# Sketched attention and a rational feed-forward in one kernel: features laid out by token, the division folded into the query features, the step order written out

## The chip, the cores and the metric

The kernel runs on one core of one Trainium2 chip. Its time is device microseconds for one execution: the median of three runs. A profile of one execution lies beside it, and all views named here are of that profile.

## What is computed

The reference, cut to what matters:

```
phi(x):  a = S1 . x ; b = S2 . x            # 8 numbers each, of 32 per head
         return outer(a, b).reshape(64)
q_p, k_p = phi(q), phi(k)                   # q, k, v: 4 batches, 4 heads, 1088 tokens, 32 wide
kv  = sum over tokens of outer(k_p, v)      # 64 x 32 per batch and head
z   = sum over tokens of k_p
x   = (q_p . kv) / (q_p . z + 1e-6)         # 4352 tokens x 128 (4 heads x 32)
h   = x @ w_in                              # 128 -> 2048
P   = a0 + a1 h + a2 h^2 + a3 h^3
Q   = 1 + |b0| |h| + |b1| h^2
out = (P / (Q + 1e-6)) @ w_out              # 2048 -> 128
```

## The kernel before, in words

**Tiling.** Of the 1088 tokens of a batch, 1024 are cut into two chunks of 512 (four blocks of 128), which makes eight chunks, n = 0 to 7. The 64 tokens left of each batch form a ninth chunk of 256, the remainder. The 2048 columns of h are 16 blocks of 128; h is kept transposed, feature on the partition and token along the row. A group is some blocks of one chunk: chunk 0 has groups of 4, 4 and 8 blocks (`FIRST`), chunks 1 to 7 two groups of 8 (4096 numbers per partition), the remainder 8, 4 and 4 blocks of 256 tokens (`LAST`).

**Keys** (`add_keys`, per batch). Per chunk, TensorE transposes four 128x128 pieces of k (L286), ScalarE copies them to SBUF (L291), TensorE multiplies by S1 and S2 together (`S12`, L296), ScalarE copies the `a` half (L303), and VectorE forms the 64 products per head in four instructions, with `b` read from PSUM (L314). TensorE accumulates k_p against v with a column of ones (`v_aug`, filled by GpSimd in L271 and L272), so that kv and z come together (L328). VectorE spreads the sums into `kv_dup` and `kv_pair` (L363, L364).

**Queries** (`add_queries`, per chunk). q is transposed (L379, L384). `Srep` expands the transposed q to `a` and to `b` repeated 64 times, features on the partition, two heads at a time (L389, a 64-row matmul); ScalarE copies the `a` side (L394), VectorE multiplies (L398): `q_pT`. TensorE forms numerators and denominators by token (L405), VectorE adds 1e-6, takes the reciprocal and multiplies (L415 to L417), TensorE transposes x (L424), ScalarE copies it (L428).

**Feed-forward** (`add_group`, per group g). h by f32 matmuls, two blocks into each of two PSUM buffers of 1024 (L466); ScalarE copies to bf16 `hb` (L472); VectorE makes |h| (L476, `m`), |b1| |h| + |b0| (L482, `u`) and u m (L486); ScalarE takes 1/Q as exp(-ln(1 + 1e-6 + u)) in pieces of 2048 (L490, L495, `r`); VectorE makes a3 h + a2 (L499, `y`), times h (L503), plus a1 (L506), times h (L503 again), times r (L510). TensorE adds two terms into the output, r against a0 w_out and y against w_out (L517), which `weights` has scaled and converted on VectorE (L258, L259). After the last group of a chunk the output is copied, transposed and stored (L522, L527, L532, L574; the remainder's four stores L580).

**Order.** Every engine carries out its instructions in the order in which they were issued. `Plan` holds steps with an engine, an assumed duration, predecessors, a rank and the buffers that they take and give; `issue` simulates them greedily with a fixed `HOP` of 190 ns between engines and issues them by start time. All loads are on SP's queue, in the order k0, S1/S2, v0, k remainders, v remainders, q0, a and b, w_in (L174), w_out (L175), then the rest (the digit is the batch). Buffers: `hb` three, `m` one, `u`, `r` and `y` two, `L` two, `xT` three, `w_ps` (PSUM for all small products) two.

The same helper makes every matmul into `w_ps`, so a line of the profile stands for one step kind. An f32 matmul appears as two records of TensorE, an f32 transpose or a bf16 matmul as one.

Of the kernel before, what the change touches and what calls it, by code (L numbers as in the profile page):

```python
# [17 lines left out]

class Plan:

    HOP = 190
# [5 lines left out]
    def add(self, engine, ns, fn, after=(), rank=0.0, take=(), give=(), lag=0):  # L30
        s = dict(engine=engine, ns=ns, fn=fn, after=[a for a in after if a is not None], rank=rank,
                 take=take, give=give, lag=lag, end=None, n=len(self.steps))
        self.steps.append(s)
        return s

    def issue(self):
        todo = list(self.steps)
        free_at = {}
        pool = {k: [0] * v for k, v in self.bufs.items()}
        done = []  # L40
        while todo:
            best = None
            for s in todo:
                if any(a["end"] is None for a in s["after"]):
                    continue
                t = free_at.get(s["engine"], 0)
                for a in s["after"]:
                    t = max(t, a["end"] + (a["lag"] if a["engine"] == s["engine"] else self.HOP + a["lag"]))
                blocked = False
                for b in s["take"]:  # L50
                    if not pool[b]:
                        blocked = True
                        break
                    t = max(t, min(pool[b]))
                if blocked:
                    continue
                key = (t, s["rank"], s["n"])
                if best is None or key < best[0]:
                    best = (key, s)
# [5 lines left out]
            for b in s["give"]:  # L65
                pool[b].append(s["end"] + self.HOP)
            todo.remove(s)
            done.append(s)
        for s in sorted(done, key=lambda s: (s["start"], s["n"])):
            s["fn"]()  # L70
# [4 lines left out]
def kernel(  # L75
# [28 lines left out]
    FR = 1.45  # L104
    GW = GF * CW
    FIRST = [4, 4, 8]
    LAST = [8, 4, 4]
# [15 lines left out]
    BUFS = dict(xT=3, hb=3, m=1, u=2, r=2, y=2, L=2, h_ps=2, out_ps=1, w_ps=2, kv_ps=1,  # L123
                k_sb=2, v_sb=2, q_sb=2, v_aug=2, kT=2, a_t=2, k_p=2, qT=2, A_sb=2, q_pT=2, den=2, x=2,
# [3 lines left out]

    k_rem = big.tile([128, B // 2, H, D], FP, name="k_rem")
    v_rem = big.tile([128, B // 2, H, D], FP, name="v_rem")
    q_rem = big.tile([128, B // 2, H, D], FP, name="q_rem")

    def load_main(name, src, b):
        t = io.tile([128, H, J, D], FP, name=name, bufs=BUFS[name])
        T[name, b] = t
        nc.sync.dma_start(out=t, in_=src[b, :, 0:MAIN, :].rearrange("h (p j) d -> p h j d", j=J))

    def load_rem(dst, src):  # L140
        for b in range(B):
            nc.sync.dma_start(out=dst[(b % 2) * REM:(b % 2 + 1) * REM, b // 2, :, :],
                              in_=src[b, :, MAIN:S, :].rearrange("h p d -> p h d"))

# [4 lines left out]
    w_out_l = moe.tile([128, LW], FP, name="L", bufs=BUFS["L"])  # L149
    w_out_f = w_out_l.rearrange("p (n d) -> p n d", d=d_model)  # L150

    def load_small():
        for i, s in enumerate((S1, S2)):
            nc.sync.dma_start(out=SR[i * R:(i + 1) * R, :, :],
                              in_=bass.AP(tensor=s.tensor, offset=s.offset, ap=[[D, R], [0, H], [1, D]]))

    def load_ab():
        nc.sync.dma_start(out=a_sb, in_=bass.AP(tensor=moe_a.tensor, offset=moe_a.offset,
                                                ap=[[0, 128]] + list(moe_a.ap)))
        nc.sync.dma_start(out=b_sb, in_=bass.AP(tensor=moe_b.tensor, offset=moe_b.offset,  # L160
                                                ap=[[0, 128]] + list(moe_b.ap)))

    def load(fn, ns, n=1, **kw):
        return plan.add("SP", 650 * n, fn, lag=ns, **kw)

    ld = {}
    ld["k", 0] = load(lambda: load_main("k_sb", k, 0), 4000, rank=-99, take=["k_sb"])
    ld["s"] = load(load_small, 2000, 2, rank=-98)
    ld["v", 0] = load(lambda: load_main("v_sb", v, 0), 4500, rank=-97, take=["v_sb"])
    ld["kr"] = load(lambda: load_rem(k_rem, k), 2500, 4, rank=-96)  # L170
    ld["vr"] = load(lambda: load_rem(v_rem, v), 2500, 4, rank=-95)
    ld["q", 0] = load(lambda: load_main("q_sb", q, 0), 4000, rank=-94, take=["q_sb"])
    ld["ab"] = load(load_ab, 2000, 2, rank=-93)
    ld["wi"] = load(lambda: nc.sync.dma_start(out=w_in_sb, in_=moe_w_in), 8000, rank=-92)  # L174
    ld["wo"] = load(lambda: nc.sync.dma_start(out=w_out_f, in_=moe_w_out.rearrange("(fo fi) d -> fi fo d", fi=128)),  # L175
                    9000, rank=-91, take=["L"])
    for i, (name, src) in enumerate((("k", k), ("v", v), ("q", q))):
        ld[name, 1] = load(lambda name=name, src=src: load_main(name + "_sb", src, 1), 6000, rank=-90 + i,
                           take=[name + "_sb"])
    ld["qr"] = load(lambda: load_rem(q_rem, q), 3000, 4, rank=-80)  # L180
    for b in range(2, B):
        for i, (name, src) in enumerate((("k", k), ("v", v), ("q", q))):
            ld[name, b] = load(lambda name=name, src=src, b=b: load_main(name + "_sb", src, b), 5000, rank=-70 + i,
                               take=[name + "_sb"])
# [5 lines left out]
    mask2 = consts.tile([128, 2], FP, name="mask2")  # L190
    one_ap = consts.tile([128, 1], FP, name="one_ap")

    kv_dup = big.tile([128, B, H, 2 * (D + 1)], FP, name="kv_dup")
    kv_pair = big.tile([128, B, NP, 2 * (D + 1)], FP, name="kv_pair")
    v_rem_aug = big.tile([128, B // 2, H, D + 1], FP, name="v_rem_aug")
# [3 lines left out]
    wide = [consts.tile([128, R, R], FP, name=f"wide{i}") for i in range(2)]  # L199
    Srep = [consts.tile([128, 2, R * R], FP, name=f"Srep{i}") for i in range(2)]  # L200
    W_terms = [big.tile([128, NF, d_model], BF, name=f"w_out_{i}") for i in range(2)]

    def pool_consts():
# [3 lines left out]
        for h in range(H):  # L207
            nc.gpsimd.memset(mask4[h * D:(h + 1) * D, h:h + 1], 1.0)
            nc.gpsimd.memset(mask2[h * D:(h + 1) * D, h % 2:h % 2 + 1], 1.0)
        nc.gpsimd.memset(one_ap, 1.0 + 1e-6)  # L210

    def pool_zero():
        nc.gpsimd.memset(kv_dup, 0.0)
        nc.gpsimd.memset(kv_pair, 0.0)
# [4 lines left out]

# [3 lines left out]
    def first_warm():  # L223
        warm_ps.append(ops.tile([128, CW], FP, name="out_ps", bufs=1))
        warm(8)

    c_zero = plan.add("DVE", 250, lambda: nc.vector.memset(zeros, 0.0), rank=-99)
    c_pool = plan.add("POOL", 2000, pool_consts, rank=-99)
    c_kv0 = plan.add("POOL", 1500, pool_zero, rank=-98)
    c_warm = plan.add("PE", 3500, first_warm, after=[c_zero], rank=-99, take=["out_ps"])  # L230

    def s_transpose():
        T["sT"] = aps.tile([128, CW], FP, name="w_ps", bufs=BUFS["w_ps"])
        nc.tensor.transpose(T["sT"][:, :2 * R], in_=SR.rearrange("r h d -> r (h d)"), identity=ident[:2 * R, :2 * R])

    def s_spread():
        nc.vector.tensor_copy(out=sT, in_=T["sT"][:, :2 * R])
        nc.vector.tensor_mul(out=S12, in0=sT[:, None, :].broadcast_to([128, H, 2 * R]),
                             in1=mask4[:, :, None].broadcast_to([128, H, 2 * R]))

    def s_rep():
        for i in range(2):
            src = sT[:, 0:R, None] if i == 0 else sT[:, None, R:2 * R]
            nc.vector.tensor_copy(out=wide[i], in_=src.broadcast_to([128, R, R]))
            nc.vector.tensor_mul(out=Srep[i],
                                 in0=wide[i].rearrange("p i j -> p (i j)")[:, None, :].broadcast_to([128, 2, R * R]),
                                 in1=mask2[:, :, None].broadcast_to([128, 2, R * R]))

    c_sT = plan.add("PE", 250, s_transpose, after=[ld["s"], c_pool], rank=-98, take=["w_ps"])
    c_s12 = plan.add("DVE", 450, s_spread, after=[c_sT], rank=-98, give=["w_ps"])  # L250
    c_rep = plan.add("DVE", 1100, s_rep, after=[c_s12], rank=-97)
# [5 lines left out]
    def weights():  # L257
        nc.vector.tensor_scalar(out=W_terms[0], in0=w_out_f, scalar1=a_sb[:, 0:1], scalar2=None, op0=AX.mult)  # L258
        nc.vector.tensor_copy(out=W_terms[1], in_=w_out_f)  # L259

    c_b = plan.add("DVE", 100, abs_b, after=[ld["ab"]], rank=-5)
    c_w = plan.add("DVE", 2500, weights, after=[ld["ab"], ld["wo"]], rank=-0.25, give=["L"])


    def add_keys(b, rank):
        warm_n = 1 if b == 0 else 0
        last = {}

        def v_ones():
            T["va", b] = io.tile([128, H, J, D + 1], FP, name="v_aug", bufs=BUFS["v_aug"])  # L270
# [3 lines left out]
        va = plan.add("POOL", 1300, v_ones, after=[ld["v", b]], rank=rank, take=["v_aug"], give=["v_sb"])  # L274
        if b == 0:
            def vr_ones():
                nc.gpsimd.memset(v_rem_aug[:, :, :, D:D + 1], 1.0)
                nc.gpsimd.tensor_copy(out=v_rem_aug[:, :, :, 0:D], in_=v_rem)

            T["vr_step"] = plan.add("POOL", 600, vr_ones, after=[ld["vr"]], rank=rank)  # L280

        def features(key, srcs, n, after, rank, give=(), keep=False):
            def transposes():
                T["kTp", key] = aps.tile([128, CW], FP, name="w_ps", bufs=BUFS["w_ps"])
# [4 lines left out]
            def evac():  # L289
                T["kT", key] = att.tile([128, CW], FP, name="kT", bufs=BUFS["kT"])  # L290
                nc.scalar.copy(out=T["kT", key][:, :n * 128], in_=T["kTp", key][:, :n * 128])  # L291

            def project_ab():
                T["ab", key] = aps.tile([128, CW], FP, name="w_ps", bufs=BUFS["w_ps"])
# [359 lines left out]
```

## Time and profile before

| what | value |
|---|---|
| median of 3 runs | 324.46 us (323.81, 324.46, 333.47) |
| profiled execution, its span | 323.9 us |
| TensorE busy | 280.0 us (86%) |
| VectorE busy | 286.5 us (88%) |
| ScalarE busy | 228.4 us (71%) |
| GpSimd busy | 8.7 us (3%) |
| mean granted TensorE clock | 0.954 |
| moved by DMA | 11.20 MB |

The page gives no time of its own for the profiled execution beside its span; against the median of the runs the span is 0.6 us shorter, which is what lies around it. Busy time is counted per engine, and the shares are of the whole span, over stages with different limits. PE is TensorE, PEld its weight loads, DVE VectorE, ACT ScalarE, POOL GpSimd, SP the queue of loads and stores.

### The profile page before, as it was taken

How to read it: one execution, taken by the hardware profiler on the slowest of the kernel's cores; microseconds unless marked ns; L12 is line 12 of the kernel's file. 1: busy time of each engine (PE TensorE's matmuls, PEld its weight loads, DVE VectorE, ACT ScalarE, POOL GpSimd, SP SyncE). 2: the span in 40 equal slices, each digit the busy share in tenths (PEclk: the TensorE clock that was granted, in tenths of full speed). 3: DMA queues.
4: the chain of work that ended last, by engine and by line, in shares of the span. 5: the costliest groups of instructions: out<-in, count | busy, mean ns of one | idle time of the engine just before them, and what ended most of it. 6: DMA issues, size and time to landing. Idle time of an engine off the chain costs nothing.

```text
span 323.9 us, 3027 instructions
## 1 busy us (share of the span) xinstructions
PE 280.0 (86%) x1153; PEld 150.0 (46%) x1172; DVE 286.5 (88%) x300; ACT 228.4 (71%) x213; POOL 8.7 (3%) x29
## 2 busy tenths in 40 slices
PE   7969999988899999898999998979999975992532
PEld 4835455555443544555445554645345422650220
DVE  1461599999999999999999999999999999999990
ACT  3122678979479879794798888675989795686650
POOL 4102000002000000000000000000000000000000
PEclk9997999999999999999999999989999999698695
DMA  5798000200020000000000000000000000000000
GB/s 157 222 314 266 0 1 2 65 1 0 25 74 0 0 34 0 0 0 2 32 0 1 34 0 0 0 2 32 0 0 35 0 0 0 0 34 0 0 32 16
DMA packets 12125, 11.20 MB, mean 35 GB/s; under 512 B 4048, under 2 KB 10448, under 8 KB 11984
## 3 DMA queue, kind: packets, MB, share of 16 engines
q1 hardware_dynamic: 12112, 11.02, 11.2%
q8 instruction: 9, 0.15, 0.2%
q14 instruction: 4, 0.03, 0.0%
HBM read 8.79 MB, written 2.23 MB: 34 GB/s over the span
## 4 chain that ended last, share of the span: by engine, by line
DVE 77%; PE 13%; DMA 5%; issue 1%; SPq 1%; ACT 1%; DVEq 0%
DVE y L503 22%; DVE u L486 11%; DVE y L510 10%; DVE y L499 6%; DVE u L482 6%; DVE y L506 6%; PE h_ps L466 6%; DVE m L476 5%; DMA L<-in_moe_w_out_dram 3%; DVE q_pT L398 3%; DVE k_p L314 2%; PE out_ps L517 2%; PE w_ps L405 2%; DMA v_sb<-in_v_dram 2%; PE w_ps L389 2%; DVE x_sb L417 2%
## 5 line engine op out<-in xcount | busy, mean ns | idle before, releaser
L466 PE MATMUL h_ps<-xT,w_in_sb 128*128 128x512 f32 (+1 forms) x288 | 127.7, 584 | 2.7 <-ACT xT L428 2.4
L472 ACT CAST hb<-h_ps 128x1024 bf16<-128x1024 f32 x68 | 67.7, 1013 | 23.6 <-PE h_ps L466 22.8
L490 ACT ACTIVATE L<-u,one_ap 128x2048 f32<-128x2048 bf16 (+1 forms) x35 | 68.4, 1954 | 18.1 <-DVE u L486 18.1
L503 DVE TENSOR_TENSOR y<-y,hb 128x4096 bf16<-128x4096 bf16 (+2 forms) x40 | 78.9, 1972 | 1.2
L466 PEld LDWEIGHTS h_ps<-xT,w_in_sb 128*128 128x128 f32 x288 | 53.3, 194 | 56.3 <-issue 42.3
L495 ACT ACTIVATE r<-L 128x2048 bf16<-128x2048 f32 (+1 forms) x35 | 65.4, 1870 | 0.4
L517 PE MATMUL out_ps<-r,w_out_108 128*128 128x512 bf16 (+1 forms) x139 | 35.6, 378 | 11.6 <-ACT r L495 11.2
L517 PE MATMUL out_ps<-y,w_out_109 128*128 128x512 bf16 (+1 forms) x132 | 34.4, 389 | 10.7 <-DVE y L510 9.9
L486 DVE TENSOR_TENSOR u<-u,m 128x4096 bf16<-128x4096 bf16 (+2 forms) x20 | 39.4, 1971 | 0.6
L510 DVE TENSOR_TENSOR y<-y,r 128x4096 bf16<-128x4096 bf16 (+2 forms) x20 | 39.3, 1965 | 0.1
L517 PEld LDWEIGHTS <-w_out_109 128*128 128x128 bf16 x144 | 14.4, 104 | 32.1 <-issue 21.7
L517 PEld LDWEIGHTS <-w_out_108 128*128 128x128 bf16 x144 | 14.2, 102 | 32.1 <-issue 22.6
L476 DVE TENSOR_SCALAR m<-hb 128x4096 int16<-128x4096 int16 (+2 forms) x20 | 21.2, 1060 | 7.5 <-ACT hb L472 7.5
L482 DVE TENSOR_SCALAR u<-m,b_abs 128x4096 bf16<-128x4096 bf16 (+2 forms) x20 | 23.7, 1185 | 0.6
L499 DVE TENSOR_SCALAR y<-hb,a_sb 128x4096 bf16<-128x4096 bf16 (+2 forms) x20 | 23.6, 1181 | 0.0
L506 DVE TENSOR_SCALAR y<-y,a_sb 128x4096 bf16<-128x4096 bf16 (+2 forms) x20 | 22.5, 1126 | 0.7
L405 PE MATMUL w_ps<-kv_dup,q_pT 128*128 128x66 f32 x128 | 16.9, 288 | 5.4 <-DVE q_pT L398 5.4
L405 PEld LDWEIGHTS w_ps<-kv_dup,q_pT 128*128 128x128 f32 x128 | 16.6, 204 | 9.7 <-DVE q_pT L398 7.7
L328 PEld LDWEIGHTS kv_ps<-v_aug,k_p 128*128 128x128 f32 x128 | 16.3, 191 | 3.2 <-issue 1.9
L394 ACT COPY A_sb<-w_ps 128x512 f32<-128x512 f32 (+1 forms) x18 | 9.5, 564 | 10.7 <-PE w_ps L389 10.7
L389 PE MATMUL w_ps<-qT,Srep_106 64*128 64x512 f32 (+1 forms) x36 | 16.9, 615 | 0.1
L328 PE MATMUL kv_ps<-v_aug,k_p 128*128 128x66 f32 x128 | 16.2, 269 | 0.1
(70 smaller groups left out, 184.0 us busy)
## 6 DMA issues: line engine op xcount, KB each, us to landing
k_sb<-in_k_dram SPq DMA_DIRECT2D x4, 512.0 KB, 4.0
v_sb<-in_v_dram SPq DMA_DIRECT2D x4, 512.0 KB, 5.8
q_sb<-in_q_dram SPq DMA_DIRECT2D x4, 512.0 KB, 3.9
out_dram<-oT SPq DMA_DIRECT2D x8, 256.0 KB, 2.0
w_in_sb<-in_moe_w_in_dram SPq DMA_DIRECT2D x1, 1024.0 KB, 7.1
k_rem<-in_k_dram SPq DMA_DIRECT2D x4, 32.0 KB, 4.4
v_rem<-in_v_dram SPq DMA_DIRECT2D x4, 32.0 KB, 2.7
q_rem<-in_q_dram SPq DMA_DIRECT2D x4, 32.0 KB, 6.4
```

The source lines that it names most:

```text
L405: nc.tensor.matmul(nd_ps[r0:r1, i * 66:(i + 1) * 66], lhsT=T["q_pT", n, hp][:, i * 128 + r0:i * 128 + r1], rhs=kv_of(b, i, hp), start=True ...
L466: nc.tensor.matmul(T["h", g, s][:, i * W:(i + 1) * W], lhsT=w_in_sb[:, fi * 128:(fi + 1) * 128], rhs=T["xT", n][:, :W], start=True, stop=True)
L472: nc.scalar.copy(out=T["hb", g][:, s * W:(s + nsub) * W], in_=T["h", g, s])
L482: nc.vector.tensor_scalar(out=T["u", g][:, :gw], in0=T["m", g][:, :gw], scalar1=b_abs[:, 1:2], scalar2=b_abs[:, 0:1], op0=AX.mult, op1=AX.add)
L486: nc.vector.tensor_mul(out=T["u", g][:, :gw], in0=T["u", g][:, :gw], in1=T["m", g][:, :gw])
L490: nc.scalar.activation(out=T["L", g, l0][:, :lw], in_=T["u", g][:, l0:l0 + lw], func=ACT.Ln, bias=one_ap)
L495: nc.scalar.activation(out=T["r", g][:, l0:l0 + lw], in_=T["L", g, l0][:, :lw], func=ACT.Exp, scale=-1.0)
L499: nc.vector.tensor_scalar(out=T["y", g][:, :gw], in0=T["hb", g][:, :gw], scalar1=a_sb[:, 3:4], scalar2=a_sb[:, 2:3], op0=AX.mult, op1=AX.add)
L503: nc.vector.tensor_mul(out=T["y", g][:, :gw], in0=T["y", g][:, :gw], in1=T["hb", g][:, :gw])
L506: nc.vector.tensor_scalar(out=T["y", g][:, :gw], in0=T["y", g][:, :gw], scalar1=a_sb[:, 1:2], scalar2=None, op0=AX.add)
L510: nc.vector.tensor_mul(out=T["y", g][:, :gw], in0=T["y", g][:, :gw], in1=T["r", g][:, :gw])
L517: nc.tensor.matmul(T["o", n][:, :W], lhsT=W_terms[t][:, fis[i], :], rhs=src[:, i * W:(i + 1) * W], start=(t == 0 and fis[i] == 0), stop=(t ...
```

## The change

**Queries by token.** q is transposed and copied as before, and then multiplied block by block by `W_abc`, 24 columns per head: S1, S2, and S2 times z reshaped, built per batch from z (`z_blocks`, `z_project`, `z_spread`; the S columns are put there by GpSimd in `s_weights`). So a token's row holds a, b and c, where a . c is the denominator. One ScalarE copy takes all of them to SBUF; VectorE forms a . c (`scale`: multiply, reduce, add 1e-6, reciprocal) and multiplies a by 1/den, and one instruction makes the 64 products of every head (`product`). TensorE transposes them back (eight 128x128 transposes, `p_transposes`), ScalarE copies them, and `x_mm` multiplies with the block-diagonal `kv_bd` as the stationary side, so that x comes out transposed; `x_mm` of head pair hp writes 64 partitions from hp * 64. Chunk 0 is made `early`: features by token without c, numerators, division and x transposes as before.

**Keys by token.** One ScalarE copy brings a and b of all four blocks to SBUF, and one instruction makes the products of a chunk (1024 numbers per partition) in place of four.

**Feed-forward.** `u` is multiplied in place, Exp writes over `u`, and `lin` takes the place of `m`; there is no `r`. `u` has three buffers, `lin` one. In even groups from g = 2 on (`THREE`), the addition of a1 is left out: hb times u goes into `hb`, y times hb into `y`, and TensorE adds a third term, hb against a1 w_out. `FIRST` is 2, 2, 4, 8 blocks, `LAST` 8, 4, 2, 2.

**Weights and loads.** a0 w_out and w_out are converted by GpSimd, a1 w_out by ScalarE. k0 is loaded in two halves; ScalarE's queue takes the first k and v remainders, a and b, and two of the last four stores.

**Order.** `ORDER`, a list of all 726 steps, is issued as written. By step, SP's queue begins

```
q0 | k0 first half | S1,S2 | k1 | k0 second half | v0 | q1 | q rem 0 | w_out | v rem 1 | v1 | k2 | w_in | v3 | k rem 1 | q3 | ...
```

and TensorE's and VectorE's queues hold, around groups 4 to 7 (`pr`, `pg`, `py` are the three terms of the output; n1, n2, n4, n5 the steps of y; * a three-term group):

```
PE:  ... h 6,6 | qptr 3,1 | pr 4,2048 | h 7,2 | h 7,0 | pg 4* | qtr 4 | kv 20 | py 4 | ktr 30 | pr 5,0 | h 7,4 | h 7,6 | ...
DVE: ... umul 5 | n4 4* | abs 6* | n4 5 | lin 6* | n5 4* | umul 6* | n5 5 | n1 6 | k product 31 | n2 6 | abs 7 | n1 7 | ...
```

The diff, cut to its core:

```diff
-    HOP = 190
+    HOP = dict(PE=220, ACT=110, DVE=110, POOL=160, SP=100)
+    SELF = dict(PE=0, ACT=60, DVE=90, POOL=60, SP=0)
...
     def issue(self):
+        if ORDER:
...
+            for i in ORDER:
...
+                self.steps[i]["fn"]()
+            return
...
-    FIRST = [4, 4, 8]
-    LAST = [8, 4, 4]
+    FIRST = [2, 2, 4, 8]
+    LAST = [8, 4, 2, 2]
+    THREE = lambda g: g >= 2 and g % 2 == 0
...
-    BUFS = dict(xT=3, hb=3, m=1, u=2, r=2, y=2, L=2, h_ps=2, out_ps=1, w_ps=2, kv_ps=1,
-                k_sb=2, v_sb=2, q_sb=2, v_aug=2, kT=2, a_t=2, k_p=2, qT=2, A_sb=2, q_pT=2, den=2, x=2,
+    BUFS = dict(xT=3, hb=3, u=3, lin=1, y=2, L=2, h_ps=2, out_ps=1, w_ps=2, kv_ps=1,
+                k_sb=2, v_sb=2, q_sb=2, v_aug=2, kT=2, ab=2, k_p=2, qT=2, abc=2, q_p=1, q_pT=2, den=2,
...
+    def s_weights(b):
+        for h in range(H):
+            nc.gpsimd.tensor_copy(out=W_abc[:, b, h, :, 0:2 * R], in_=S12)
+        for i in range(b, B, 2):
+            nc.gpsimd.tensor_copy(out=W_rem[:, i, :, 0:2 * R], in_=S12)
...
-        nc.vector.tensor_scalar(out=W_terms[0], in0=w_out_f, scalar1=a_sb[:, 0:1], scalar2=None, op0=AX.mult)
-        nc.vector.tensor_copy(out=W_terms[1], in_=w_out_f)
+    c_w0 = plan.add("POOL", 2300, lambda: nc.gpsimd.tensor_scalar(
+        out=W_terms[0], in0=w_out_f, scalar1=a_sb[:, 0:1], scalar2=None, op0=AX.mult),
+        after=[ld["ab"], ld["wo"]], rank=-4)
+    c_w1 = plan.add("POOL", 2300, lambda: nc.gpsimd.tensor_copy(out=W_terms[1], in_=w_out_f), after=[ld["wo"]], rank=-3.9)
+    c_w2 = plan.add("ACT", 1900, lambda: nc.scalar.activation(
+        out=W_terms[2].rearrange("p n d -> p (n d)"), in_=w_out_l, func=ACT.Copy, scale=a_sb[:, 1:2]),
...
+                nc.vector.tensor_mul(out=k_p, in0=ab[:, :, 0:R, None].broadcast_to([128, n * H, R, R]),
+                                     in1=ab[:, :, None, R:2 * R].broadcast_to([128, n * H, R, R]))
...
+        def kv_blocks():
+            nc.vector.tensor_mul(out=kv_bd[:, b, :, 0:2 * D].rearrange("p n (h d) -> p n h d", h=2),
+                                 in0=kv_of()[:, :, :, 0:D],
+                                 in1=mask2[:, None, :, None].broadcast_to([128, NP, 2, D]))
...
+        def z_blocks():
+            nc.vector.tensor_mul(out=z_bd[:, b], in0=kv_of()[:, :, 0, D:D + 1].broadcast_to([128, NP, 2 * R]),
+                                 in1=mask16[:, None, :].broadcast_to([128, NP, 2 * R]))
...
+            nc.tensor.matmul(T["zp", b][:, :H * R], lhsT=S2x, rhs=z_bd[:, b].rearrange("p n c -> p (n c)"),
+                             start=True, stop=True)
...
+                nc.vector.tensor_mul(out=W_abc[:, b % 2, :, :, 2 * R:R3], in0=z[:, :, None, :].broadcast_to([128, H, JC, R]),
+                                     in1=mask4[:, None, :, None].broadcast_to([128, H, JC, R]))
...
+        def project():
+            T["abcp", n] = tile_of(aps, "w_ps", [128, CW], FP)
+            for (c0, c1, g0, w) in weights():
+                r0 = c0 % 128
+                nc.tensor.matmul(T["abcp", n][r0:r0 + c1 - c0, g0 * RC:(g0 + 4) * RC], lhsT=T["qT", n][:, c0:c1],
+                                 rhs=w.rearrange("p g r -> p (g r)"), start=True, stop=True)
...
+        def scale():
...
+            nc.vector.tensor_mul(out=pr, in0=abc[:, :, 0:R], in1=abc[:, :, 2 * R:R3])
+            nc.vector.tensor_reduce(out=den, in_=pr, axis=mybir.AxisListType.X, op=AX.add)
+            nc.vector.tensor_scalar(out=den, in0=den, scalar1=1e-6, scalar2=None, op0=AX.add)
+            nc.vector.reciprocal(out=den, in_=den)
+            nc.vector.tensor_mul(out=abc[:, :, 0:R], in0=abc[:, :, 0:R], in1=den.broadcast_to([128, G, R]))
...
+        def x_mm(hp):
...
+            for (c0, c1, w) in kv_lhs(hp):
+                nc.tensor.matmul(T["xTp", n][hp * 64:(hp + 1) * 64, c0:c1], lhsT=w[:, 0:2 * D],
+                                 rhs=T["q_pT", n][:, hp, c0:c1], start=True, stop=True)
...
+        if terms == 2:
+            p = plan.add("DVE", ts, n_add, after=[p], rank=g - 0.3, name=f"n3 {g}")
+            p = plan.add("DVE", tt, mul(y, y, hb), after=[p], rank=g - 0.3, give=["hb"], name=f"n4 {g}")
+            p = plan.add("DVE", tt, mul(y, y, u), after=[p, e], rank=g + 0.55, name=f"n5 {g}")
...
+        else:
+            r = plan.add("DVE", tt, mul(hb, hb, u), after=[p, e], rank=g + 0.5, name=f"n4 {g}")
+            p = plan.add("DVE", tt, mul(y, y, hb), after=[r], rank=g + 0.55, name=f"n5 {g}")
+            o = plan.add("PE", pj, lambda: project("hb", 2, 0, len(fis), False, False), after=[r, rt, c_w], rank=g + 0.55,
+                         give=["u"], name=f"pg {g}")
+            o = plan.add("PE", pj, lambda: project("y", 1, 0, len(fis), False, final), after=[p, o], rank=g + 0.56,
+                         give=["hb", "y"], name=f"py {g}")
...
-            nc.sync.dma_start(out=out[b * S + MAIN:(b + 1) * S, :],
-                              in_=oT[(b % 2) * REM:(b % 2 + 1) * REM, b // 2, :])
+            (nc.sync if b % 2 == 0 else nc.scalar).dma_start(
+                out=out[b * S + MAIN:(b + 1) * S, :], in_=oT[(b % 2) * REM:(b % 2 + 1) * REM, b // 2, :])
```

## The prediction, made before the changed kernel ran

> **What bounds the kernel now.** First the page's busy table and its 40 slices.
>
> ```profile
> span 323.9 us, 3027 instructions
> PE 280.0 (86%) x1153; PEld 150.0 (46%) x1172; DVE 286.5 (88%) x300; ACT 228.4 (71%) x213; POOL 8.7 (3%) x29
> PE   7969999988899999898999998979999975992532
> DVE  1461599999999999999999999999999999999990
> ```
>
> VectorE (DVE) has little to do for four slices and is then full to the end: its idle time is the start and the last few us. But TensorE (PE) is nearly full too, until the last eight slices. How nearly is read from busy time by window, in two chunks of the steady part with one batch of keys:
>
> ```profile
> core 0: us, PE busy (x) PEld busy (x) DVE busy (x) ACT busy (x) POOL busy (x), PEclk, DMA share, GB/s
> 131.00:197.00 66.00, 62.90 (x262) 33.42 (x266) 65.04 (x64) 52.60 (x51) 0.00 (x0) 1.00 0.02 9
> ```
>
> DVE 98.5%, PE 95.3%, ScalarE (ACT) 80%. A saving on DVE alone can thus give at most some 5% here. Next the timeline of the start:
>
> ```profile
> 9.93 0.43 SPq L174 DMA_DIRECT2D w_in_sb<-in_moe_w_in_dram  x1
> ...
> 20.54 1.29 DVE L258 TENSOR_SCALAR w_out_108<-L,a_sb 128x2048 bf16<-128x2048 f32 x1 [2.27 <-DMA L<-in_moe_w_out_dram]
> ...
> 23.00 1.29 DVE L398 TENSOR_TENSOR q_pT<-A_sb,w_ps 128x512 f32<-128x512 f32 x2
> ...
> 30.98 7.13 PE L466 MATMUL h_ps<-xT,w_in_sb 128*128 128x512 f32 x16
> ...
> 35.77 0.69 DVE L476 TENSOR_SCALAR m<-hb 128x2048 int16<-128x2048 int16 x1 [7.49 <-ACT hb L472]
> ```
>
> The feed-forward stream of DVE starts at 35.77: the weight copies (L258, L259) wait for w_out and hold up q_pT, and so x and h. From 35.7 to 316.5 DVE is busy 275.15 of 280.8 us (98.0%); 7.4 us follow. So the span is 35.8 + 280.7 + 7.4, and I price the three parts.
>
> **DVE work, whole run.** Rows by form (mean ns last before the second bar):
>
> ```profile
> L506 DVE TENSOR_SCALAR y<-y,a_sb 128x4096 bf16<-128x4096 bf16 x15 | 19.3, 1286 | 0.5
> L314 DVE TENSOR_TENSOR k_p<-a_t,w_ps 128x256 f32<-128x256 f32 x32 | 11.2, 415 | 1.2 <-ACT a_t L303 1.2
> L398 DVE TENSOR_TENSOR q_pT<-A_sb,w_ps 128x512 f32<-128x512 f32 x16 | 10.3, 683 | 0.1
> L245 DVE TENSOR_TENSOR Srep_107<-wide_105,mask_96 128x128 f32<-128x128 f32 x1 | 0.3, 293 | 0.0
> ```
>
> Third term: n_add (L506) goes in seven groups of 4096 (9.0 us), two of 2048 (0.75 each) and one of 512 (about 0.35): -10.9. Finer first and last groups: a two-term group of 1024 costs 4.76 us over its eight rows, one of 2048 7.96, so two for one is +1.56; at 512, by the slope between 1024 and 2048, 3.15, so +1.54: +3.1. Key products: L398 gives 1.05 ns per element (683 at 512, 414 at 256), so one product of 1024 takes 1.22; eight are 9.8 against 11.2: -1.4. Queries: lines 398 and 415 to 417 go, 25.0 in all their forms; new per later chunk are two multiplies of 128 elements (0.29, L245), the reduction, an addition (0.16) and a reciprocal (0.20) as before, and a product of 1.22. No row shows a reduction; it lies between a 64-wide copy (0.22) and twice the multiply (0.58); I take 0.29 because it reads as many elements. That is 2.45 times seven, 2.8 for chunk 0 (old division), 1.7 for the remainder: 21.7, so -3.3 (+2 at the upper bound). kv: twelve copies of 0.22 per two batches become four or five multiplies per batch: 5.4 to 4.3, -1.1. Weights and Srep gone, S2x copied: -3.2. Sum -16.8: 269.7 us. Of this about 10.4 lies before the stream (five key products, query 0, S and kv blocks) where it was 11.36, so 259.3 us follow.
>
> In the two-chunk window: -2.57 (n_add), -0.4, -0.8, -0.3: DVE 65.04 to 61.0.
>
> **PE work, the same window.** Rows of that window:
>
> ```profile
> L389 PE MATMUL w_ps<-qT,Srep_106 64*128 64x512 f32 x8 | 4.5, 641 | 0.0
> L405 PE MATMUL w_ps<-kv_dup,q_pT 128*128 128x66 f32 x32 | 3.9, 275 | 0.6 <-DVE q_pT L398 0.6
> L389 PE MATMUL w_ps<-qT,Srep_107 64*128 64x512 f32 x8 | 2.4, 635 | 0.0
> L424 PE MATMUL w_ps<-ident,x_sb 128*128 128x128 f32 x8 | 1.2, 276 | 0.1
> ```
>
> These 12.0 us go (an f32 matmul is two records). Added: 8 projections of 96 columns at 0.29 (64 columns, L296, take 0.26): 2.3; 16 transposes of q_p at 0.15: 2.4; one z projection 0.3; the third term, 16 bf16 matmuls at the 0.216 between starts of L517: 3.5. The last is x_mm, four f32 matmuls 64 outputs wide on 512 columns. L389, half an array high, shows both ends: two halves one after the other 1.05 us each, both together 1.06. Which holds for half-width tiles is shown by the remainder's numerators, which write 64 outputs each into alternating halves:
>
> ```profile
> L405 PE MATMUL w_ps<-kv_pair,q_pT 128*64 128x66 f32 x16 | 0.7, 228 | 0.0
> ```
>
> 0.044 us a record against 0.12 for the full-width ones: halves run together. The new order puts the two x_mm of most chunks side by side, so I take 2.1 (two pairs), 4.2 as the other end. PE 62.9 - 12.0 + 10.6 = 61.5 (or 63.6). So **the third term hands PE what the shorter query path saved**, and DVE and PE become equal.
>
> [...]
>
> **How fast a window becomes.** DVE at today's 98.5%: 62.0 us. PE at today's 95.3%: 64.5, or 66.7 with 63.6. Two equal engines wait for each other more than one behind a full one, so I take 64.5. ACT gains an evacuation of 384 elements per chunk (about 0.48; 512 take 0.59) and 0.1 per key chunk: 54 of 64.5, inside its gaps. Cover gone, it would cost that 0.6 a chunk.
>
> **The start.** On SP's queue the order is q0, half of k0, S1/S2, k1, the other half, v0, q1, one q remainder, w_out, a v remainder, v1, k2, and only then w_in: 5.5 MiB with itself, about 6.0 MB with the remainders. k2 waits for k_sb, which the transposes of k0 free by about 9, earlier than the bandwidth. DMA moved 231 and 283 GB/s in 2 to 6 us and 305 to 347 in 14 to 22: 1.0 MB by 6 us and 5.0 at 310 give w_in at about 22 (21 to 25), later than today's 17.0. What else h waits for: v0 (2 MiB) at about 9.7, its copy 11, key sums to 16, numerators, two divisions of 0.8, transposes and evacuation, about 21. So w_in ends last. The k and v remainders and a, b are issued by ACT (six issues, 0.6 each on SP today) while it has nothing to evacuate (until 6.10 today); the k remainder, first in PE's order, lands at 7 to 8, under v0's 11. The third weight copy (2048 wide, about 1.9 as L495) falls in ACT's wait for w_in. The other two copies go to POOL; w_out lands near 16 and its first copy takes 2 to 4 us (v_aug: 1.04 for half as many elements), ahead of the W_abc copies (about 2) that z_spread waits for on DVE: 20 to 22, under w_in; from 25 on it would be late, and the stream behind it with it. h at 22.0, and the first 1024 columns evacuated 3.05 us later, as now (30.98 to 34.02): **the stream starts at 25.1, not 35.8**.
>
> **The end.** 7.4 us: the last projection halves (-0.4), and four stores whose issue took 2.46 on one queue go by two (-1.2): 5.8.
>
> **Sum.** 25.1, plus 3.5 windows of 64.5 (225.8), plus the other 259.3 - 3.5 x 61.0 = 45.8 us of DVE at 98% (46.7), plus 5.8: 303.4 against 323.9. The median of the runs lies 0.6 above that span, so about **304**; its own range is 294 (DVE sets the window, w_in at 21) to 314 (66.7, w_in at 25).
>
> **Rivals.**
> (1) PE becomes the bound: x_mm one after the other, 63.6 a window at 95.3%: 3.5 x 2.2 = 8 us more, **312**. For: PE has no slack left. Against: the kv_pair row.
> (2) The start gives nothing, because w_in behind k2, or the W_abc copies behind POOL's weight copies, come as late as x does today: 304 + 10.7 = **315**. Against: 5.5 MiB at any rate seen after 14 us.
> (3) Slower: the hold on hb. A three-term group writes hb times u into hb and needs it until n5, where today the second L503 releases it; with three hb the evacuation for group g+3 waits for that, and ACT's Ln behind it, and PE's h. In the new order 9.4 us of DVE work lie between n5 of group 4 and abs of group 7, and in that time PE must do py 4 (1.8), a key transpose (0.6), a projection (0.9) and two h of 1.72, and ACT the last evacuation: 8.3 us. From 1.1 us of delay on DVE stands still; 4 us in each of seven groups make 28, **332**. For: PE full and in order. Against: DVE's only wait for hb now is the first, 7.5 us.
> (4) The gains add undisturbed, 62.0 a window or better: **294** or below.
>
> **How the numbers follow.** Forecast 0.55, (1) 0.16, (2) 0.08, (3) 0.13, (4) 0.08. A difference under 2% is about what cannot be told from none; the bounds are 318 and 331. The forecast, (4), and most of (1) and (2) lie under 318: 0.77; same takes 0.12, from what is left of (1) and (2) and a half-paid (3); slower 0.11, the rest of (3). The range, 293 to 321, leaves out the slower half of (3) and the tail of (4).
>
> **What would show it.** First DVE work on h near 25 us; w_in landing last before h; a two-chunk window of 64 to 65 us with PE and DVE both at 94 to 96%; pairs of x_mm in about 1.1 us; DVE busy about 270 us. I am wrong on the mechanism if PE idles over 10% in the middle while DVE waits for hb, or if DVE stays over 98% and yet takes 66 us a window.

## The result, and the profile after

The changed kernel takes **308.97 us** (median; 304.52 to 310.27), the kernel before beside it 324.13: ratio **0.948** [0.939, 0.957]. Run again unchanged later (`e12`), it took 305.97 us, ratio 0.941 [0.936, 0.947]. The profiled execution of the changed kernel took 310.27 us, the slowest of its four, and that of `e12` 305.65; the table gives both. The forecast was 304 us: faster, as expected, and near. But two of its three terms were wrong, in opposite directions:

| part of the span | before | forecast | after | `e12` |
|---|---|---|---|---|
| to the first VectorE work on h | 35.8 | 25.1 | 43.4 | 42.3 |
| the stream, to the last step of y | 280.7 | 272.5 | 259.1 | 255.9 |
| the end | 7.4 | 5.8 | 5.8 | 5.6 |
| span | 323.9 | 303.4 | 308.3 | 303.7 |

The start became 8 us longer instead of 11 shorter; the stream, which is VectorE's part from the first work on h to the last step of y, lost 21.6 us instead of 8.2. The page of the changed kernel ("after" from here on), busy table and slices:

```profile
span 308.3 us, 3083 instructions
PE 287.0 (93%) x1189; PEld 163.1 (53%) x1189; DVE 268.5 (87%) x253; ACT 234.9 (76%) x228; POOL 16.9 (5%) x45
...
PE   5999999999999999999999999999999997977962
...
DVE  0237349999999999999999999999999998999892
```

VectorE now has little to do for six slices, and TensorE counts as busy in all of them but the first. What TensorE does there shows in the timeline of the start (start, duration, engine, line; in brackets what the engine waited for):

```profile
18.42 0.38 ACTq L212 DMA_DIRECT2D a_sb<-in_moe_a_dram  x1
18.59 3.52 PE L396 MATMUL kv_ps<-v_aug,k_p 128*128 128x66 f32 x16
...
23.38 5.44 POOL L320 TENSOR_SCALAR w_out<-L,a_sb 128x2048 bf16<-128x2048 f32 x1 [11.11 <-DMA a_sb<-in_moe_a_dram]
...
23.78 5.06 DVE L316 TENSOR_SCALAR b_abs<-b_sb 128x2 int32<-128x2 int32 x1 [2.42 <-DMA b_sb<-in_moe_b_dram]
...
38.59 3.76 PE L616 MATMUL h_ps<-xT,w_in_sb 128*128 128x512 f32 x4
...
43.43 0.55 DVE L653 TENSOR_SCALAR y<-hb,a_sb 128x1024 bf16<-128x1024 bf16 x1 [3.09 <-ACT hb L622]
```

Three things are to be seen. The 16 key sums take 3.52 us, where `e12` does the same 16 in 1.90, and the four records of h 3.76, where they take 1.88 later on: TensorE runs at half rate. The load of a is issued only at 18.42, and GpSimd's copy of a0 w_out waits for it. And `b_abs`, two numbers per partition, takes 5.06 us beside that copy (0.17 before). In the stream the picture is the reverse; busy time by window, and after it VectorE's waits between 60 and 290 us (us in total, times, longest):

```profile
core 0: us, PE busy (x) PEld busy (x) DVE busy (x) ACT busy (x) POOL busy (x), PEclk, DMA share, GB/s
131.00:197.00 66.00, 65.73 (x289) 35.18 (x288) 65.31 (x62) 60.43 (x57) 0.00 (x0) 1.00 0.02 9
```

```profile
DVE y L653 <- PE out_ps L662: 1.3, 2, 1.0
```

Both engines stand at 99%, and VectorE waits 1.3 us for others in 230. The first y step of the 4096-wide groups starts at 155.95 and, two chunks (four groups) later, at 218.59: **62.6 us for two chunks**. Before, the same distance was 66.2 (160.57 to 226.76).

### The profile page after: what moved, and what is told of

It reads as the page before. It is cut to its first block, busy times and chain, and to the rows that moved or that the text cites. A ratio compares the mean times of both kernels' runs of the same rounds, so it can differ in the third digit from the quotient of the medians.

```text
span 308.3 us, 3083 instructions
## 1 busy us (share of the span) xinstructions
PE 287.0 (93%) x1189; PEld 163.1 (53%) x1189; DVE 268.5 (87%) x253; ACT 234.9 (76%) x228; POOL 16.9 (5%) x45
## 4 chain that ended last, share of the span: by engine, by line
DVE 47%; PE 43%; issue 4%; ACT 3%; DMA 2%; DVEq 0%
DVE y L642 18%; PE h_ps L616 14%; PE out_ps L662 12%; DVE u L642 6%; DVE lin L638 5%; PE kv_ps L396 5%; DVE y L653 5%; DVE hb L642 4%; DVE u L633 4%; PE w_ps L362 3%; DVE y L656 2%; DVE q_p L515 2%; DMA k_rem<-in_k_dram 2%; PE w_ps L479 1%; PE w_ps L352 1%
## 5 line engine op out<-in xcount | busy, mean ns | idle before, releaser
L622 ACT CAST hb<-h_ps 128x1024 bf16<-128x1024 f32 (+1 forms) x69 | 68.4, 999 | 24.5 <-PE h_ps L616 21.3
L616 PEld LDWEIGHTS h_ps<-xT,w_in_sb 128*128 128x128 f32 x288 | 53.9, 197 | 48.4 <-issue 39.5
L642 DVE TENSOR_TENSOR y<-y,hb 128x4096 bf16<-128x4096 bf16 (+3 forms) x44 | 78.7, 1798 | 0.1
L646 ACT ACTIVATE L<-u,one_ap 128x2048 f32<-128x2048 bf16 (+2 forms) x37 | 69.2, 1870 | 6.6 <-DVE u L642 6.2
L649 ACT ACTIVATE u<-L 128x2048 bf16<-128x2048 f32 (+2 forms) x37 | 65.8, 1779 | 0.3
L662 PEld LDWEIGHTS <-w_out 128*128 128x128 bf16 x358 | 35.5, 100 | 57.2 <-issue 31.1
L662 PE MATMUL out_ps<-y,w_out 128*128 128x512 bf16 (+1 forms) x144 | 34.7, 381 | 5.5 <-DVE y L642 5.5
L662 PE MATMUL out_ps<-u,w_out 128*128 128x512 bf16 (+1 forms) x144 | 36.7, 383 | 3.4 <-ACT u L649 3.4
L642 DVE TENSOR_TENSOR u<-lin,u 128x4096 bf16<-128x4096 bf16 (+3 forms) x22 | 39.6, 1799 | 0.1
L653 DVE TENSOR_SCALAR y<-hb,a_sb 128x4096 bf16<-128x4096 bf16 (+3 forms) x22 | 24.2, 1098 | 5.9 <-ACT hb L622 3.1
L638 DVE TENSOR_SCALAR lin<-u,b_abs 128x4096 bf16<-128x4096 bf16 (+3 forms) x22 | 24.1, 1097 | 0.1
L362 PEld LDWEIGHTS w_ps<-S,kT 128*128 128x128 f32 x68 | 12.6, 262 | 2.3 <-issue 1.5
```

The lines of the kernel that those rows point to most:

```text
L362: nc.tensor.matmul(T["abp", key][:, i * 64:(i + 1) * 64], lhsT=T["kT", key][:, i * 128:(i + 1) * 128], rhs=S12.rearrange("p h r -> p (h r) ...
L616: nc.tensor.matmul(T["h", g, s][:, i * W:(i + 1) * W], lhsT=w_in_sb[:, fi * 128:(fi + 1) * 128], rhs=T["xT", n][:, :W], start=True, stop=True)
L622: nc.scalar.copy(out=T["hb", g][:, s * W:(s + nsub) * W], in_=T["h", g, s][:, :nsub * W])
L638: nc.vector.tensor_scalar(out=lin(), in0=u(), scalar1=b_abs[:, 1:2], scalar2=b_abs[:, 0:1], op0=AX.mult, op1=AX.add)
L642: return lambda: nc.vector.tensor_mul(out=out(), in0=in0(), in1=in1())
L646: nc.scalar.activation(out=T["L", g, l0][:, :lw], in_=T["u", g][:, l0:l0 + lw], func=ACT.Ln, bias=one_ap)
```

## The experiments

**`e12`, `e10`, `e1`, `e5`: what holds the start.** `e12` is the changed kernel unchanged, once more. `e10` only issues a and b right behind the first remainders on ScalarE's queue, ahead of its evacuations; `e1` only doubles the dummy matmuls of the start; `e5` does both.

In short (the steps of the queue by name; a and b are one step):

```diff
 e1, e5:  first_warm:  -        warm(7)
                       +        warm(14)
 e10, e5: ORDER, ACT:  - k rem 0 | v rem 0 | eight evacuations | a, b | ...
                       + k rem 0 | v rem 0 | a, b | eight evacuations | ...
```

> The first run of dummy matmuls is 14 long in place of 7, so that it bridges the gap until the k remainder arrives (4.43 to 6.56 us in the profile of the changed kernel). Theory A (clock): the changed kernel's start is late because TensorE's matmuls run at half rate from 6.56 to 42 us (16 key-sum records take 3.5 us where the kernel before took 1.9); with the gap bridged the first of them are at full rate, the feed-forward stream of VectorE starts at 28 to 35 us in place of 43.4, and the time falls by 5 to 12 us to about 297. Theory B (loads and waits): the start hangs on the k remainder, v0, and a, b behind GpSimd's weight copy; then the stream still starts at 41 to 44 and the time stays within 3 us of 307.

> The 14 first dummy matmuls, and a and b are loaded on ScalarE's queue right behind the first remainders, in place of behind nine evacuations; nothing else. In the kernel with the 14 alone, the block-diagonal kv copies on VectorE end at 23.33 us, when GpSimd's 5.44 us weight copy ends, and TensorE stands for 3.1 us before the numerators and is then at half rate. Theory A (the late a, b): VectorE's b_abs no longer waits, GpSimd's copy starts when w_out lands (about 17), the kv copies come at 20 or, still held by the copy, at 22.6; stream at 28 to 34, time 296 to 303. Theory B (only the copy on GpSimd counts, not when a and b arrive): the kv copies are held to 22.5 or later, stream at 34 to 35.5, within 1.5 us of the kernel with the 14 alone (303).

> The changed kernel with a and b loaded early and nothing else: the first dummy matmuls stay 7 long. Theory A (the clock is the larger loss, and the late a, b count only behind it): matmuls at half rate from 6.6 to about 40 us as in the changed kernel, stream at 40 to 43, time 304 to 307. Theory B (the late a, b are the loss, and the half rate only follows from the wait that they cause): stream at 28 to 34, time 294 to 300.

> The changed kernel once more, unchanged, to see whether the same list of instructions starts at the same clock each time. Theory A (the clock's release in the first 45 us is a matter of chance, since the kernel with early a and b had it at 13 us and the changed kernel's profile not before 42): the executions spread over 5 us or more, 302 to 309, more than those of the kernels with a bridged gap (1.1 to 1.8 us with early a and b). Theory B (each list of instructions has one start): the executions agree within 2 us.

| kernel | median us (lowest to highest) | ratio to before | stream starts | stream |
|---|---|---|---|---|
| after | 308.97 (304.52 to 310.27) | 0.948 [0.939, 0.957] | 43.4 | 259.1 |
| `e12` | 305.97 (304.84 to 309.71) | 0.941 [0.936, 0.947] | 42.3 | 255.9 |
| `e1` | 303.24 (301.85 to 303.67) | 0.927 [0.918, 0.935] | 35.5 | 258.8 |
| `e10` | 296.78 (295.37 to 309.61) | 0.913 [0.906, 0.921] | 30.4 | 258.8 |
| `e5` | 294.37 (293.66 to 295.36) | 0.910 [0.907, 0.912] | 28.4 | 258.7 |

The start moves by 15 us, and the stream behind it stays at 256 to 259: the two terms add, as in the sum of the prediction. The second theory for `e10` came true. `e5` started where its first theory said and was 1.6 us faster than that theory's range; `e1` fell between its two theories, and so did `e12`, whose six executions spread over 4.9 us. `e12` shows how the loads of a and b hold the start, even where the keys run at full rate. Its timeline and, behind it, its windows:

```profile
15.90 0.36 ACTq L212 DMA_DIRECT2D a_sb<-in_moe_a_dram  x1
15.90 1.90 PE L396 MATMUL kv_ps<-v_aug,k_p 128*128 128x66 f32 x16
...
24.53 5.44 POOL L320 TENSOR_SCALAR w_out<-L,a_sb 128x2048 bf16<-128x2048 f32 x1 [11.94 <-DMA v_sb<-in_v_dram]
24.94 5.05 DVE L316 TENSOR_SCALAR b_abs<-b_sb 128x2 int32<-128x2 int32 x1 [6.11 <-DMA b_sb<-in_moe_b_dram]
...
30.15 3.65 PE L541 MATMUL w_ps<-kv_bd,q_pT 128*128 128x66 f32 x16 [7.68 <-DVE kv_bd L440]
...
38.14 3.04 PE L616 MATMUL h_ps<-xT,w_in_sb 128*128 128x512 f32 x4
...
42.27 0.55 DVE L653 TENSOR_SCALAR y<-hb,a_sb 128x1024 bf16<-128x1024 bf16 x1 [2.37 <-ACT hb L622]
```

```profile
24.00:32.00 8.00, 1.85 (x9) 1.88 (x10) 5.05 (x3) 2.00 (x1) 7.47 (x9) 0.67 0.02 4
32.00:40.00 8.00, 8.00 (x34) 6.96 (x34) 4.44 (x11) 1.33 (x3) 3.35 (x11) 0.50 0.00 0
```

a is issued at 15.90 and lands 8.5 us later by the DMA view, among the large loads (the page names v as what the copy waited for; a landed last). Copy and `b_abs` then end together at 30 (in after, `e1` and `e2` too they end within 0.03 us of each other, however late `b_abs` began), `kv_bd` is queued behind `b_abs` on VectorE, TensorE stands for 7.68 us and comes back at a granted clock of 0.50, at which what leads to h takes about twice as long (numerators 3.65 us, 1.97 in `e5`; transposes of x 1.06, 0.61 in `e5`). In `e5` the same rows read:

```profile
16.76 0.17 DVE L315 TENSOR_SCALAR b_abs<-b_sb 128x2 int32<-128x2 int32 x1
...
18.48 5.44 POOL L319 TENSOR_SCALAR w_out<-L,a_sb 128x2048 bf16<-128x2048 f32 x1 [4.66 <-DMA L<-in_moe_w_out_dram]
...
20.00 0.29 DVE L435 TENSOR_TENSOR kv_bd<-kv_ps,mask 128x128 f32<-128x128 f32 x1 [3.08 <-PE kv_ps L395]
...
25.31 1.96 PE L615 MATMUL h_ps<-xT,w_in_sb 128*128 128x512 f32 x4
...
28.36 1.85 DVE L652 TENSOR_SCALAR y<-hb,a_sb 128x1024 bf16<-128x1024 bf16 x1 [1.31 <-ACT hb L621]
```

`b_abs` is done ahead of the copy, `kv_bd` runs in its usual 0.29 beside it, and h begins at 25.31 in place of 38. `e10` shows that the early a and b do most of it alone (stream at 30.4, 12 us before `e12`); the dummies alone bring 6.8 us of the start and 2.7 of the time (`e1`, 303.24 beside `e12`'s 305.97), because there `b_abs` still ends with the copy, at 23.3, TensorE still stands 3.1 us, and its first h records still take 3.76. What is **not settled** is why the keys ran at half rate in after's profiled execution and at full rate in `e12`'s, which issues the same instructions: with seven dummies the executions spread widely (304.5 to 310.3; one run of `e10` at 309.61 among three at 295 to 297), with fourteen under 2 us in `e1` and `e5` but over 8 in `e2`, below. So it varies by execution, and the number of dummies alone doesn't settle it.

**`e2`: more dummies between the small steps.** `e1`, with one more dummy matmul behind each projection of keys and behind the first query transposes, and new ones among the key sums and behind the numerators.

> As with the 14 first dummy matmuls, and the dummy matmuls between the small ones of batch 0 and chunk 0 are put back in the numbers of the kernel before (two after each projection of keys, one before each of the eight pairs of key sums, two after the first query transposes and after each half of the numerators). Theory A (clock): small f32 matmuls alone do not keep the clock up, so this start is at full rate throughout: stream at 26 to 30 us, time 292 to 299, at least 3 us below the kernel with the 14 first ones alone. Theory B (loads and waits): about 18 more dummy matmuls are work in a start that waits for something else, 0 to 4 us more than the changed kernel.

301.6 us (295.04 to 303.16), no interval; the profiled stream starts at 39.5 and takes 256.2. Beside `e1`'s 303.24 the median is no clear gain: three executions took 301.0 to 303.2, and only one, at 295.04, lies in the range of theory A. Theory A's premise does not hold in `e5`: from 13.92 us to h at 25.31 its small f32 matmuls run without a dummy among them and stay at full rate (16 key sums 1.90 us, the numerators 1.97). In the profiled execution of `e2`, 303.16, the wait for a and b is still there: copy and `b_abs` end at 25.4, TensorE stands 3.1 us behind them and goes on at half rate. So neither theory is settled.

**`e6`, `e9`: what is left of the start.** `e6` is `e5` with the copy of a0 w_out on VectorE, behind `b_abs`; `e9` is `e6` with k1 behind v0 instead of ahead of it, and w_in right behind w_out, on SP's queue.

```diff
-    c_w0 = plan.add("POOL", 2300, lambda: nc.gpsimd.tensor_scalar(
+    c_w0 = plan.add("DVE", 1300, lambda: nc.vector.tensor_scalar(
```

> As the one before, and the first weight copy (a0 w_out) is taken from GpSimd and put on VectorE, right before the kv copies. If GpSimd's 5.44 us copy holds VectorE's instructions for as long as it runs, this frees 2.5 to 3.5 us: kv copies end at about 20.3, TensorE goes on at full rate, the stream starts at 27 to 30, time 292 to 297. If GpSimd's copy holds nobody, the 1.3 us on VectorE are added and the time is that of the kernel before it or 1 us more.

> The kernel with 14 first dummy matmuls, early a and b and the first weight copy on VectorE (293.6), and on SP's queue k1 moved behind v0, and w_in ahead of the second remainders, v1 and k2, so that nothing in front of it waits for a buffer. If loads still bind its start (v0's copy at 11 to 12, w_in's landing near 24), the stream starts at 25.5 to 27.5 in place of 28.7 and the time falls by 1 to 3 us. If TensorE's chain of small steps binds it (features, key sums, numerators, division, all at full rate), the stream stays within 0.7 us of 28.7 and the time within 1 us.

293.56 us, ratio 0.907 [0.905, 0.909], and 293.57, ratio 0.905 [0.899, 0.910]; the streams start at 28.7 and 28.3. The copy costs 1.3 us on VectorE in place of 5.4 on GpSimd, but in `e5` it already held nobody on the way to x, so the 2.5 to 3.5 us of the first expectation for `e6` don't come: moving it brings 0.8 us, within the spread of the two. That much shows in the first step of y, which took 1.85 us in `e5` beside GpSimd's plain cast of w_out (28.04 to 29.93) and takes 0.55 in `e6`, where the cast is done by 23.4. Loading w_in earlier brings no time either, as the second expectation for `e9` said: h begins 0.9 us sooner (24.77, 25.67 in `e6`), but the plain cast now falls beside the key product ahead of the first y, which takes 2.71 us in place of 1.23. What is left of the start is the chain of small steps: TensorE is busy for 26.3 of its 28.7 us in `e6`. These are the **fastest versions**, 12 to 15 us under the two medians of the changed kernel. The page of `e6`:

```profile
span 292.1 us, 3077 instructions
PE 271.0 (93%) x1179; PEld 149.2 (51%) x1196; DVE 264.9 (91%) x254; ACT 234.9 (80%) x228; POOL 13.8 (5%) x44
```

TensorE's busy time falls from 287.0 to 271.0 although it got more dummies, and the instructions of after took 275.1 in `e12`: much of the 93% in after was work at half rate.

**`e4`: the same steps in the planner's order.** `ORDER = []`, so that `issue` sets the order greedily.

> The changed kernel with an empty list of steps, so that its own planner (the greedy simulation with the new hops) sets the order; everything else is as in the changed kernel. If the gain is in the work taken off VectorE, this keeps most of it: 305 to 315. If the gain is in the written-out order of steps, it is lost: 318 to 328.

323.66 us, ratio 0.988 [0.977, 1.000], as the second expectation has it. The stream starts at 35.2 and takes **282.6**, against 259.1 under the list and 280.7 before. Its VectorE waits between 60 and 300 us:

```profile
DVE u L601 <- ACT hb L590: 16.9, 6, 5.2
DVE den L474 <- ACT abc L465: 2.8, 1, 2.8
DVE k_p L349 <- ACT ab L338: 2.0, 2, 1.4
DVE W_abc L426 <- PE w_ps L417: 1.9, 1, 1.9
DVE y L610 <- ACT u L617: 1.6, 1, 1.6
```

VectorE's busy time is 265.1 us, no more than after's 268.5. So the work that the change took off VectorE came back as waits, most of them for hb, and the stream was no shorter than before; the order is what turns saved work into saved time. The order without the saved work was not run; it had little to take, because before, VectorE was idle for under 6 of the 280.8 us of the stream.

**`e3`, `e7`, `e8`: the third term.** `e3`: no group has it (`THREE = lambda g: False`), each even group's four steps at the same places of the list, in order of dependence. `e7`: the same under the planner's order. `e8`: the kernel before, with the third term in even groups from 2 on (a1 w_out and hb r on VectorE).

```diff
 e8:
+        three = g >= 2 and g % 2 == 0
...
+            nc.vector.tensor_mul(out=T["hb", g][:, :gw], in0=T["hb", g][:, :gw], in1=T["r", g][:, :gw])
...
-            src = T["r", g] if t == 0 else T["y", g]
+            src = T[("r", "y", "hb")[t], g]
```

> The changed kernel with two output terms in every group: the a1 addition is back on VectorE in all groups, 10.9 us in all, and TensorE loses 60 matmuls of 512 columns and 10 of 256, about 14 us; the order is the same but for the four steps of y in each of these groups, which stand in their order of dependence. Theory A (VectorE sets the stream, TensorE has room): 9 to 11 us slower, 316 to 318. Theory B (both are full, and TensorE is what the stream waits for): under 5 us slower.

> The changed kernel with an empty list of steps (the planner's own order) and two terms in every group; to be compared with the same order rule with the third term (323.7 us), so that no list that was made for the other form is in the way. Theory A (VectorE sets the stream): 9 to 12 us slower than that, 333 to 336. Theory B (TensorE is what such an order waits for): between 4 faster and 4 slower, 320 to 328.

> The third term alone: the kernel before, with hb times r, y times hb and a third projection in even groups from g = 2, and the third weight copy on VectorE (1.3 us at the start). VectorE loses about 10 us in all and gains 1.3, TensorE gains about 14 us, with the longer query path still on it. Theory A (both engines are full, and the third term only pays with the shorter query path): 321 to 330, no gain. Theory B (VectorE alone sets the time): 8 to 10 us faster, 314 to 316.

| kernel | median us | ratio to before | stream or two chunks |
|---|---|---|---|
| `e3` | 326.18 | 1.001 [0.996, 1.005] | stream 274.7; two chunks 65.8 |
| `e7` | 323.23 | 0.996 [0.992, 1.001] | stream 280.9 |
| `e8` | 336.99 | 1.041 [1.039, 1.044] | two chunks 71.7 |

Only `e7` came out as one of its theories (B) said; `e3` and `e8` are slower than both of theirs. Under the list the third term is worth 15.6 us of stream, more than the 10.9 of n_add that it removes; but the list was made for it, so that `e3` also measures a list that doesn't fit. Under the planner's order it is worth nothing (`e7` against `e4`). Put into the kernel before, it costs 4%. The window of `e8` that the prediction read for before:

```profile
131.00:197.00 66.00, 63.28 (x252) 33.64 (x254) 57.42 (x59) 48.27 (x47) 0.00 (x0) 0.95 0.02 9
```

VectorE falls to 87% there (98.5% before), with TensorE at 96%, and between 100 and 300 us it waits for ScalarE:

```profile
DVE hb L515 <- ACT r L497: 9.1, 2, 6.1
DVE m L478 <- ACT hb L474: 6.7, 1, 6.7
```

Neither is the slower rival's hold on hb. The first is hb times r, which needs r two steps sooner than y times r does in the kernel before. In the second, at 184.47, ScalarE's evacuations wait for h, which TensorE begins at 176.26, when x has just come (175.05); no evacuation between 100 and 300 us waits for a free hb. Beside these waits stands a TensorE with a third term more and no lighter query path to pay for it. How much of the 4% is the planner's order and how much TensorE's load, no run tells.

## Why the prediction was right, and where it was not

That the total came out is luck: the start was forecast 18.3 us too short and the stream 13.4 too long (17.2 and 16.6 by `e12`).

**"The stream starts at 25.1", "w_in ends last": wrong by 18 us.** w_in had landed by about 24, when the DMA traffic ends in after, inside the range that I gave, and loading it earlier moved the start by 0.4 us (`e9`). What ended last was TensorE's chain to x. Four things were mis-sized. (a) a and b: I saw that they go to ScalarE's queue "while it has nothing to evacuate", but by the list they stand behind eight evacuations, issued at 18.42, not by 6. That is worth 12 us (`e10`). (b) GpSimd's first weight copy, taken at 2 to 4 us, took 5.44, and I did not ask who else stands still meanwhile; `b_abs` did, for 5.06 us. The row for v_aug, a plain copy, was the wrong neighbour: the plain cast of the same 2048 numbers (L323) took 1.90. (c) TensorE's rate: my durations came from rows at full rate, but behind seven dummies and an idle gap of 2.14 us four transposes of k took 1.06 us in after, 0.60 in `e5`, which has fourteen dummies and no such gap; and behind the gap for `kv_bd` the numerators took 3.65 in `e12`, 1.97 in `e5`. (d) The rest, 3.3 us, is still there in `e5`: h at 25.3, not 22.0. I let the key sums end at 16; the first 16 do (13.92 to 15.82), but the second chunk's and the remainder's end at 19.9. Evacuation of the first h: 3.05 expected, 3.05 found (25.31 to 28.36).

What brings the rate down and back up, the runs show only in part. In `e12` TensorE stands for 7.68 us and comes back at a granted clock of 0.50; from 30.15 to about 41 us it is then busy without a gap, at a mean granted clock of 0.53. Nor does the recorded clock show every half rate: in after's profile the column shows 1.00 through the first 54 us, while the first four records of h, at 38.59, take 3.76 us in place of 1.88.

**"Two equal engines wait for each other more than one behind a full one, so I take 64.5": wrong.** Two chunks take 62.6, close to the 62.0 that I gave for VectorE alone at today's 98.5%, with both engines at 99%. `e4` shows waits of 25 us under an order found greedily, 282.6 us of stream; the written order leaves 1.3 us of waits in 230. So in the stream rival (4), undisturbed gains, is what happened, and the start hid it in the total. Of the stream's 13.4 us under the forecast, 5.5 are VectorE time (253.8 busy against 259.3 priced) and 7.9 idle time (5.3 against 13.2).

**DVE work, "Sum -16.8": right as a sum of rows.** Added up, VectorE's rows come to 295.7 us before and 283.1 after: -12.6, or -17.5 without the 4.9 that `b_abs` lost. The new rows by form (total, mean ns, idle before it):

```profile
L515 DVE TENSOR_TENSOR q_p<-abc 128x1024 f32<-128x1024 f32 x8 | 9.7, 1218 | 0.0
L381 DVE TENSOR_TENSOR k_p<-ab 128x1024 f32<-128x1024 f32 x8 | 9.7, 1218 | 3.9 <-ACT ab L370 3.9
L510 DVE TENSOR_TENSOR abc<-abc,den 128x128 f32<-128x128 f32 x7 | 2.0, 292 | 0.2
L507 DVE TENSOR_REDUCE den<-den 128x16 f32<-128x128 f32 x7 | 2.0, 288 | 0.2
```

1.22 for the products, 0.29 for the multiplies and for the reduction, as priced. Busy time fell by more than the rows, 18.0 or 22.9 without `b_abs`: instructions that follow without a wait overlap in the records, the rows by 9.2 us before and by 14.6 after. Most of the 5.5 above is this.

**PE work: "pairs of x_mm in about 1.1 us": right.** Alone, and two side by side (the timeline in the stream):

```profile
88.79 1.07 PE L535 MATMUL w_ps<-q_pT,kv_bd 128*64 128x512 f32 x2
...
149.38 1.14 PE L535 MATMUL w_ps<-q_pT,kv_bd 128*64 128x512 f32 x4
```

Half-width tiles in alternate halves run together, four records in 1.14 us where two alone take 1.07, so that rival (1) had no ground. "The third term hands PE what the shorter query path saved" fits both engines at 99%, and `e8`, where nothing was saved, is slower.

**The slower rival, hb: not paid.** VectorE does not wait for hb anywhere between 60 and 290 us in after. The hold itself shows there once, on ScalarE, where an evacuation waits for a three-term group's last projection to free hb; a second one waits for VectorE:

```profile
ACT hb L622 <- PE out_ps L662: 1.6, 1, 1.6
ACT hb L622 <- DVE y L642: 1.2, 1, 1.2
```

Neither reached VectorE, so the 1.1 us of margin that I worked out by hand was enough under the list. In `e4` VectorE waits for hb for 16.9 us, but in `e7`, where no group has a third term, it does so too:

```profile
DVE u L601 <- ACT hb L590: 12.2, 3, 5.9
```

In both the evacuations wait for h from TensorE, and none between 60 and 300 us for a free hb. These waits come with the greedy order, not from the third term's hold.

**The end: right**, 5.8 us. **"The median of the runs lies 0.6 above that span": too little**: after's profiled execution took 310.27 us at a span of 308.3, `e12`'s 305.65 at 303.7, so some 2.0 lie around it. I had set the span of one execution of before against the median of others.

## What to carry to other kernels

Follow each small load and each tiny instruction of a start to the engine queue in which it stands, and ask what is queued behind it: three kilobytes of coefficients issued late, and one instruction of two elements per partition held by a copy on another engine, cost 12 us here. Price a stream and its order separately: the same instructions took 282.6 us in a greedy order and 259.1 in the written one, and less work on the fullest engine became less time only in the second. When a forecast of the total comes true, compare its terms all the same; here errors of 18 and 13 us in opposite directions nearly cancelled.

## What the runs showed of the hardware

- `b_abs`, a VectorE instruction on two numbers per partition, takes 5.06 us where it falls beside a GpSimd TENSOR_SCALAR of 5.44 (after), and 0.17 ahead of it (`e5`); `kv_bd`, with one operand in PSUM, takes 0.29 beside the same copy (`e5`). Why the one is held and the other not, no run shows. Where the copy came during a VectorE product (`e10`), the copy took 6.00 and `b_abs`, next behind the product, 0.16. Larger instructions are held as well: a key product took 2.49 us in place of 1.22 beside GpSimd's plain cast, which took 2.91 in place of 1.90 (`e10`).
- GpSimd's TENSOR_SCALAR with a factor per partition, 2048 numbers f32 to bf16, takes 5.44 us, the plain cast 1.90 (both in after); on VectorE the first takes 1.29 (before).
- A 2 KB load issued at 4.49 us among the large ones landed after 2.8 us (`e10`); issued at 18.42 (after) and 15.90 (`e12`) it took 4.9 and 8.5, and landed at 23.3 and 24.4, as the large ones ended.
- TensorE can show as busy without a gap for over 10 us and stay at half rate: in `e12` it is busy for 10.85 of the 10.85 us from 30.15 to 41, at a mean granted clock of 0.53.
